# A polynomial-sketch attention with a multiplicative FFN: new float64 conversion, token-major query features and a reordered program

## The chip, the cores and the metric

The kernel runs on one core of one Trainium2 chip. The metric is the device time of one execution in microseconds (us); for a kernel run several times, the median of its runs. Engines: PE is TensorE's matmul, PEld its weight load, DVE is VectorE, ACT is ScalarE, POOL is GpSimd, SP is SyncE, which issues all DMAs here (SPq is its queue).

## The reference

Two parts. The attention maps each query and key x of 32 numbers to 64 features, the outer product of S1 x and S2 x (8 each); with kv = sum of features(k) times v over the tokens and z = sum of features(k), each token and head gets x = (features(q) kv) / (features(q) z + 1e-6). There are 4 batches, 4 heads, 1088 tokens. The four heads of 32 side by side are the 128 numbers of a token for the FFN.

```python
def phi(x):
    a = np.einsum('rd,bhsd->bhsr', S1, x)
    b = np.einsum('rd,bhsd->bhsr', S2, x)
    return np.einsum('bhsi,bhsj->bhsij', a, b).reshape(*x.shape[:-1], r * r)
q_p, k_p = (phi(q), phi(k))
kv = np.einsum('bhsf,bhsd->bhfd', k_p, v)
z = np.sum(k_p, axis=2)
num = np.einsum('bhsf,bhfd->bhsd', q_p, kv)
den = np.einsum('bhsf,bhf->bhs', q_p, z)[..., None] + 1e-06
...
a = x @ w1
b = x @ w2
h = a * b @ w3
return (h @ w_out).astype(np.float32)
```

x is 4352 x 128; w1 and w2 are 128 x 1024, w3 is 1024 x 1024, w_out 1024 x 128. S1, S2 and the four weights arrive as float64; q, k, v are float32. The denominator is a sum with signs that can nearly cancel, so the kernels carry it in pairs of float32 (a leading part on a coarse grid, exact in products and sums, and the rest).

## The kernel before, in words

Tokens are cut into 9 groups: two of 512 for each batch (`q_main`), and one of 256 with the last 64 tokens of each batch (`q_rest`). Since no nonlinearity stands between w3 and w_out, w3o = w3 w_out is computed once (`w3_t` transposes w3 on TensorE, `w3_mm` multiplies by w_out), and a group's FFN is 8 column steps: a product with w1 (`mlp_steps`, L592), ScalarE's copy to SBUF, a product with w2 (L596), VectorE's product of both (ab, L598), and three steps (LAG) later the product with w3o (L605), summed over the 8 steps; then ScalarE copies it (ob), TensorE transposes it (ps_ot), and it is stored.

The weights are loaded as 64-bit words in 22 chunks of 128 x 512 (raw, 4 buffers) in the order w_out, w3, w1, w2. `split_words` (L200 to L220) makes float32 of a chunk: ScalarE scales the low words (L209), VectorE masks, clips, shifts and joins the high words (L211 to L216, six steps), GpSimd multiplies (L217) and `convert` adds the two parts on GpSimd (L306).

Keys, for each batch (`k_steps`): 8 chunks of 128 tokens in two halves of four, and the remaining 64 tokens. For each half TensorE transposes the keys (ps_kt), ScalarE copies (kT), TensorE multiplies by S1 and S2 (ps_ab), VectorE forms the features (kp, L376). `gram` then issues for each chunk two products of kp with v (L412), and three products of the keys' leading part k1 and rest k2 (L416 to L418). `fin1` to `fin3` turn the sums into the matrix M of the denominator, in small VectorE steps between small products (ps_T, ps_M).

Queries, for each group (`q_steps`), with tokens along the free axis: transposes (qT); leading part q1 and rest q2 (GpSimd, L501); two feature products (ps_w, L510) with ScalarE's copy and VectorE's product qp (L523); M q in three products (ps_y, L532 to L534); VectorE's split of it and four GpSimd steps (L540 to L543); numerator and denominator (ps_nd, L552 to L555), the reciprocal between two VectorE transposes, and x (xT).

The program is one list of steps: `merge` interleaves streams by their given costs, and a scheduler then orders each engine's queue. Before the first FFN group stand keys of batches 0 and 1, queries of batch 0 and all of the weights; each batch's two FFN groups are merged with the keys two batches on and the queries one batch on. PSUM: three banks (tag h) for the FFN and the weights, one (t) for transposes, one for the key sums, two (w2) for the queries, one for the FFN's sum.

Of the kernel before, what the change touches and what calls it, by code (L numbers as in the profile page):

```python
# [713 lines left out]
```

## Time and profile before

| what | us |
|---|---|
| median of 3 runs | 427.97 |
| lowest and highest run | 427.85 and 437.18 |
| span of the profiled execution | 425.6 |
| PE busy in it | 356.6 |
| DVE busy | 250.5 |
| POOL busy | 138.3 |
| ACT busy | 98.2 |

The span runs from the first to the last instruction of the profiled execution; the runs' times are those of whole executions and lie 2.4 us above it. Busy times overlap, so they don't add up to the span.

### The profile page before, as it was taken

To read this page: it belongs to the slowest core of one execution; us is meant where nothing else is said; L and a number is where in the kernel's file an instruction comes from. 1 tells how busy PE (TensorE), PEld (TensorE's weight loads), DVE (VectorE), ACT (ScalarE), POOL (GpSimd) and SP (SyncE) were. 2 spreads that over 40 slices of the span, in tenths; PEclk is the share of its full clock that TensorE was granted. 3 is DMA by queue.
4 is the path that set the end of the run, shared out by engine and by line. 5 is a ranking of instruction groups with operands and counts; after the bars stand their busy time and mean duration, and the time that the engine had idled before them with its cause. 6 is when DMAs were issued, how large, how long until landed. Compare 5 with 4: busy or idle time off the path is not lost.

```text
span 425.6 us, 4174 instructions
## 1 busy us (share of the span) xinstructions
PE 356.6 (84%) x1432; PEld 210.7 (50%) x1432; DVE 250.5 (59%) x552; ACT 98.2 (23%) x176; POOL 138.3 (33%) x106
## 2 busy tenths in 40 slices
PE   0665645738788398999999999999999999999994
PEld 0465644626588234364645464464544444445563
DVE  5994499956978997446255643516744554424321
ACT  1212013412032131204211311411221411322231
POOL 0666195394637457051050131104014113002000
PEclk9995658668988689999999999999999999999998
DMA  5986083240227030003000000000000000000001
GB/s 113 259 150 207 12 223 98 65 147 1 69 81 199 1 49 0 2 0 49 26 0 0 2 25 0 0 26 0 0 27 1 0 25 2 0 25 0 26 0 37
DMA packets 44116, 20.71 MB, mean 49 GB/s; under 512 B 37184, under 2 KB 40512, under 8 KB 44096
## 3 DMA queue, kind: packets, MB, share of 16 engines
q1 hardware_dynamic: 44096, 20.46, 18.9%
q8 instruction: 11, 0.18, 0.2%
q14 instruction: 9, 0.07, 0.1%
HBM read 18.22 MB, written 2.23 MB: 48 GB/s over the span
## 4 chain that ended last, share of the span: by engine, by line
PE 70%; DVE 14%; SPq 6%; issue 4%; POOL 4%; ACT 1%; DMA 1%; POOLq 0%; DVEq 0%
PE b_ps L596 14%; PE ps_o L605 14%; PE a_ps L592 14%; PE ps_w L510 4%; SPq L100 4%; PE ps_kvz L412 2%; DVE cv_c L211 2%; PE ps_y L533 2%; DVE cv_a L214 2%; PE ps_w3o L332 2%; DVE cv_a L215 2%; PE ps_y L534 2%; PE ps_nd L554 2%; PE ps_kvz L416 2%; PE ps_ab L368 2%
## 5 line engine op out<-in xcount | busy, mean ns | idle before, releaser
L598 DVE TENSOR_TENSOR ab<-ffa,b_ps 128x512 f32<-128x512 f32 (+1 forms) x72 | 47.2, 656 | 68.5 <-PE b_ps L596 63.5
L592 PE MATMUL a_ps<-xT,w 128*128 128x512 f32 (+1 forms) x144 | 71.8, 580 | 1.2 <-POOL w L306 1.2
L596 PE MATMUL b_ps<-xT,w 128*128 128x512 f32 (+1 forms) x144 | 70.9, 574 | 0.0
L92 ACT COPY ffa<-a_ps 128x512 f32<-128x512 f32 (+1 forms) x72 | 40.5, 563 | 119.5 <-PE a_ps L592 117.5
L605 PE MATMUL ps_o<-ab,w3o 128*128 128x512 f32 (+1 forms) x144 | 67.4, 571 | 0.0
L217 POOL TENSOR_TENSOR cv_m<-cv_m,cv_c 128x512 f32<-128x512 f32 (+1 forms) x23 | 37.2, 1622 | 43.6 <-DVE cv_c L216 26.1
L324 PE MATMUL ps_wt<-ident,w3c 128*128 128x128 f32 x64 | 14.2, 350 | 36.7 <-POOL w3c L306 36.7
L605 PEld LDWEIGHTS ps_o<-ab,w3o 128*128 128x128 f32 x144 | 27.0, 190 | 30.3 <-issue 28.5
L596 PEld LDWEIGHTS b_ps<-xT,w 128*128 128x128 f32 x144 | 27.0, 192 | 28.0 <-issue 27.1
L501 POOL TENSOR_TENSOR q<-qT,q 128x512 f32<-128x512 f32 (+1 forms) x9 | 12.4, 1381 | 84.3 <-DVE q L235 67.4
L540 POOL TENSOR_TENSOR p<-q,yh 128x512 f32<-128x512 bf16 (+1 forms) x9 | 10.0, 1112 | 86.0 <-DVE yh L235 86.0
L592 PEld LDWEIGHTS a_ps<-xT,w 128*128 128x128 f32 x144 | 24.9, 190 | 25.6 <-issue 19.3
L324 PEld LDWEIGHTS ps_wt<-ident,w3c 128*128 128x128 f32 x64 | 9.7, 182 | 39.6 <-POOL w3c L306 39.6
L209 ACT ACTIVATE cv_m<-raw 128x512 f32<-128x512 uint32 x22 | 14.6, 677 | 63.2 <-POOL w3c L306 58.1
L227 DVE TENSOR_REDUCE g_y<-ps_y 128x1 f32<-128x512 f32 (+1 forms) x9 | 5.9, 661 | 31.5 <-PE ps_y L534 31.5
L412 PE MATMUL ps_kvz<-v_sb,kp 128*128 128x64 f32 x128 | 20.3, 287 | 4.5 <-DVE kp L376 4.5
L332 PE MATMUL ps_w3o<-wo,w3T 128*128 128x128 f32 x128 | 23.0, 348 | 0.0
L412 PEld LDWEIGHTS ps_kvz<-v_sb,kp 128*128 128x128 f32 x128 | 19.5, 216 | 6.6 <-DVE kp L376 5.2
L332 PEld LDWEIGHTS ps_w3o<-wo,w3T 128*128 128x128 f32 x128 | 21.9, 260 | 0.5 <-issue 0.5
L306 POOL TENSOR_TENSOR w3c<-cv_a,cv_m 128x512 f32<-128x512 f32 x16 | 21.6, 1353 | 1.0
L392 POOL TENSOR_TENSOR k<-k_sb,k 128x512 f32<-128x512 f32 x8 | 10.3, 1304 | 27.8 <-DVE k L235 27.8
L214 DVE SCALAR_TENSOR_TENSOR cv_a<-cv_c,cv_a 128x512 int32<-128x512 int32 (+1 forms) x23 | 18.6, 818 | 0.0
(167 smaller groups left out, 559.6 us busy)
## 6 DMA issues: line engine op xcount, KB each, us to landing
raw<-in_moe_w_dram SPq DMA_DIRECT2D x20, 512.0 KB, 4.0
k_sb<-in_k_dram SPq DMA_DIRECT2D x16, 128.0 KB, 3.7
v_sb<-in_v_dram SPq DMA_DIRECT2D x4, 512.0 KB, 4.9
q_sb<-in_q_dram SPq DMA_DIRECT2D x16, 128.0 KB, 3.8
out_dram<-oT SPq DMA_DIRECT2D x8, 256.0 KB, 2.0
raw<-in_moe_w_out_dram SPq DMA_DIRECT2D x2, 512.0 KB, 4.8
kr<-in_k_dram SPq DMA_DIRECT2D x4, 32.0 KB, 2.3
vr<-in_v_dram SPq DMA_DIRECT2D x4, 32.0 KB, 2.7
```

The source lines that it names most:

```text
L92: nc.scalar.copy(dst, src)
L100: nc.sync.dma_start(t[:, :, h], bass.AP(tensor=src.tensor, offset=(b * H + h) * S * D, ap=[[NJ * D, 128], [D, NJ], [1, D]]))
L214: nc.vector.scalar_tensor_tensor(a, ci, 0x40000000, a, ALU.bitwise_and, ALU.bitwise_or)
L217: nc.gpsimd.tensor_mul(m, m, c)
L306: nc.gpsimd.tensor_add(dst, hi_f, m)
L324: nc.tensor.transpose(ps[:, c], w3c[:, c * 128:(c + 1) * 128], ident)
L332: nc.tensor.matmul(ps, t[:, c], wo[:, c], start=(c == 0), stop=(c == NC - 1))
L412: nc.tensor.matmul(kv_ps[:, p], kp_chunk[rows, 2 * p:2 * p + 2].rearrange("s h i j -> s (h i j)"), vt[rows, 2 * p:2 * p + 2], start=first ...
L592: nc.tensor.matmul(a_ps[:, :n], w1[:, cols], xT[key], start=True, stop=True)
L596: nc.tensor.matmul(b_ps[:, :n], w2[:, cols], xT[key], start=True, stop=True)
L598: nc.vector.tensor_mul(ab[:, :n], a_sb[:, :n], b_ps[:, :n])
L605: nc.tensor.matmul(s["o"][:, :n], w3o[:, c], s["ab"].pop(c)[:, :n], start=c == 0, stop=c == NC - 1)
```

## The change

`split_words` with its six VectorE steps stays for S1 and S2 alone. The weights get a conversion of their own:

```python
    def convert(n, dst):
        lo, hi = halves(raw.pop(n), CW)
        ...
        nc.scalar.mul(c, hi.bitcast(F32), 2.0 ** -112)
        nc.scalar.mul(m, lo.bitcast(U32), 2.0 ** -29)
        top = HI_TOP * 2.0 ** -112
        nc.vector.tensor_scalar(c, c, top, -top, ALU.min, ALU.max)
        ci = c.bitcast(I32)
        nc.vector.tensor_scalar(t, ci, 3, 0x7FFFFFF8, ALU.logical_shift_left, ALU.bitwise_and)
        nc.vector.scalar_tensor_tensor(t, ci, -(1 << 31), t, ALU.bitwise_and, ALU.bitwise_or)
        nc.vector.tensor_tensor(dst.bitcast(I32), t, m, ALU.add)
        load_raw(n + 1 + NRAW)
```

[...] raw has 6 buffers, and the chunks come in the order w1, w2, w_out, w3.

```diff
-        v_sb[b] = io.tile([128, H, NJ, D], F32, tag="v", name="v_sb")
-        nc.sync.dma_start(v_sb[b].rearrange("p h j d -> p h (j d)"),
-                          bass.AP(tensor=v.tensor, offset=b * H * S * D,
-                                  ap=[[NJ * D, 128], [S * D, H], [1, NJ * D]]))
+        v_sb[b] = io.tile([128, NJ, H, D], F32, tag="v", name="v_sb")
+        load_main(v_sb[b], v, b)
```

So v is loaded as k is, in four DMAs of runs of 32 numbers. Keys: the leading part k1 is bfloat16, GpSimd makes the sum ks = k + k1, and one product of k2 and ks stands for two:

```diff
-                nc.tensor.matmul(kv_ps[:, p],
-                                 kp_chunk[rows, 2 * p:2 * p + 2].rearrange("s h i j -> s (h i j)"),
-                                 vt[rows, 2 * p:2 * p + 2],
+                nc.tensor.matmul(acc["kv"][64 * p:64 * (p + 1)], vt[rows, 2 * p:2 * p + 2].rearrange("p h d -> p (h d)"),
+                                 kp_chunk[rows, 2 * p:2 * p + 2].rearrange("s h i j -> s (h i j)"),
...
-            nc.tensor.matmul(g2_ps, k1[rows], k2[rows], start=False, stop=False, skip_group_check=True)
-            nc.tensor.matmul(g2_ps, k2[rows], kf[rows], start=False, stop=last, skip_group_check=True)
+            nc.tensor.matmul(acc["g2"], k2[rows], ks[rows], start=False, stop=last, skip_group_check=True)
```

Queries: `ay` has the queries as weights (128 tokens at a time, q1 in bfloat16, q2 and qT in float32) and 64 to 96 columns that hold S1, S2 and the key sums of the denominator, so that tokens lie along the partitions. `split` and `dens` form the denominators and 1/den in VectorE steps of 128 to 256 elements per partition, `phi` the features with 1/den in them, `phT` transposes them (8 transposes of 128, ScalarE's copy pT), and `nd` multiplies by kv (ps_x, two products side by side) and ScalarE copies x. The fused FFN functions are as before but for LAG, which is 10 steps counted over all groups, and the order:

```diff
-    run(merge(rest_steps(0, "t") + k_steps(0, "t") + q_main(0, 0, "t") + k_steps(1, "t") + q_main(0, 1, "t"),
-              setup_steps()))
...
+    run(merge(rest_steps(0) + k_steps(0) + q_main(0, 0), weight_steps(("w1", "w2"))))
+    w_st = weight_steps(("wo", "w3"))
+    cut = len(w_st) // 2
+    run(merge(ffn_steps(0), q_main(0, 1), w_st[:cut]))
+    run(merge(ffn_steps(1), k_steps(1) + q_main(1, 0), w_st[cut:]))
+    run(merge(ffn_steps(2), q_main(1, 1), rest_steps(1) + k_steps(2)))
```

SP's queue, from its start: s_raw are the sketches, kr and vr the remaining tokens, raw the words of the weights. Before:

```order
L161 DMA s_raw<-in_S_dram 8x32 x2
L100 DMA k_sb<-in_k_dram 128x8x32 x4
L115 DMA v_sb<-in_v_dram 128x4x256
L105 DMA kr_67<-in_k_dram 64x4x32 x2
L105 DMA vr_71<-in_v_dram 64x4x32 x2
L157 DMA raw<-in_moe_w_out_dram 128x4x128 x2
L100 DMA q_sb<-in_q_dram 128x8x32 x4
L157 DMA raw<-in_moe_w_dram 128x512 x2
```

Now:

```order
L144 DMA s_raw<-in_S_dram 8x32 x2
L85 DMA k_sb<-in_k_dram 128x8x32 x4
L85 DMA v_sb<-in_v_dram 128x8x32 x4
L90 DMA kr_67<-in_k_dram 64x4x32 x2
L90 DMA vr_71<-in_v_dram 64x4x32 x2
L85 DMA q_sb<-in_q_dram 128x8x32 x4
L140 DMA raw<-in_moe_w_dram 128x512 x4
L140 DMA raw<-in_moe_w_out_dram 128x4x128 x2
L85 DMA k_sb<-in_k_dram 128x8x32 x4
```

The words of w1 and w2 come first among the weights, but all raw words now stand behind q, and v is four DMAs instead of one.

TensorE's queue where the FFN starts. Before, with ps_wt and ps_w3o (w3's transposes and products) ahead of the first a_ps, and ps_T and ps_M of key batch 1 around it:

```order
L324 MATMUL ps_wt<-ident,w3c 128x128 x2
L332 MATMUL ps_w3o<-wo,w3T 128x128 x6
L257 MATMUL ps_T<-P1s,gb 128x32
L332 MATMUL ps_w3o<-wo,w3T 128x128 x2
L592 MATMUL a_ps<-xT,w_73 128x512
L255 MATMUL ps_M<-Ta,Pl_blk 128x32
L256 MATMUL ps_M<-Tb,Pl_blk 128x32
L257 MATMUL ps_M<-Ts,Pr_blk 128x32
L496 MATMUL ps_qt<-ident,q_sb 128x128 x4
```

Now, from the first query group's transposed features (ps_ph) and x (ps_x) on:

```order
L584 MATMUL ps_ph<-ident,ph 128x128 x8
L602 MATMUL ps_x<-pT,kz_406 64x512 x2
L498 MATMUL ps_qt<-ident,q_sb 128x128 x4
L646 MATMUL a_ps<-xT,w_73 128x512
L650 MATMUL b_ps<-xT,w_74 128x512
L646 MATMUL a_ps<-xT,w_73 128x512
L650 MATMUL b_ps<-xT,w_74 128x512
L327 MATMUL ps_wt<-ident,w3c 128x128 x4
```

The first FFN products stand ahead of every w3 transpose, behind key batch 0 and one query group alone.

VectorE's queue at a conversion. Before, two chunks at a time, between kp and the next key step:

```order
L376 TENSOR_TENSOR kp<-ps_ab,b_sb 128x1024
L211 TENSOR_SCALAR cv_c<-raw 128x512 x2
L212 TENSOR_SCALAR cv_c<-cv_c 128x512 x2
L213 TENSOR_SCALAR cv_a<-cv_c 128x512 x2
L214 SCALAR_TENSOR_TENSOR cv_a<-cv_c,cv_a 128x512 x2
L215 SCALAR_TENSOR_TENSOR cv_a<-raw,cv_a 128x512 x2
L216 TENSOR_SCALAR cv_c<-cv_a 128x512 x2
L235 TENSOR_SCALAR k_387<-k_sb,g_kb 128x512
```

Now, after the first kp (ISA is the integer add, whose rows count half-words):

```order
L383 TENSOR_TENSOR kp<-ps_ab,b_sb 128x1024
L212 TENSOR_SCALAR cv_c<-cv_c 128x512
L214 TENSOR_SCALAR cv_t<-cv_c 128x512
L215 SCALAR_TENSOR_TENSOR cv_t<-cv_c,cv_t 128x512
L216 ISA w_73<-cv_t,cv_m 128x1024
L212 TENSOR_SCALAR cv_c<-cv_c 128x512
L214 TENSOR_SCALAR cv_t<-cv_c 128x512
L215 SCALAR_TENSOR_TENSOR cv_t<-cv_c,cv_t 128x512
```

Six steps per chunk became four, one of them of a new kind; nine of the 22 adds stand ahead of the FFN's first step on this queue.

## Rows read from the trace of the kernel before

**Rows 1.** Stretches: us, busy us (x instructions) by engine, PEclk, DMA share, GB/s.
```profile
30.00:75.00 45.00, 23.19 (x124) 21.53 (x124) 33.52 (x62) 8.73 (x16) 26.63 (x18) 0.65 0.48 133
75.00:150.00 75.00, 50.36 (x297) 41.51 (x299) 61.95 (x129) 18.63 (x35) 43.69 (x30) 0.80 0.28 78
150.00:419.00 269.00, 267.83 (x938) 134.43 (x934) 130.24 (x269) 64.17 (x112) 54.87 (x47) 1.00 0.05 12
```

**Rows 2.** Waits from 0 to 150 us: who for whom, us in total, times, longest.
```profile
ACT cv_m L209 <- POOL w3c L306: 58.1, 13, 19.0
PE ps_wt L324 <- POOL w3c L306: 36.7, 11, 10.1
```

**Rows 3.** Time line of PE, first FFN product: start, us, what (x instructions).
```profile
151.64 1.06 PE L596 MATMUL b_ps<-xT,w 128*128 128x512 f32 x1
```

**Rows 4.** Time line of PE at the full clock, 238 to 262 us.
```profile
238.59 0.60 PE L496 MATMUL ps_qt<-ident,q_sb 128*128 128x128 f32 x4
239.02 1.02 PE L592 MATMUL a_ps<-xT,w 128*128 128x512 f32 x2
...
240.50 1.13 PE L510 MATMUL ps_w<-qT,Sa 64*128 64x512 f32 x4
241.56 1.10 PE L368 MATMUL ps_ab<-S12blk,kT 128*128 128x64 f32 x8
242.50 1.08 PE L596 MATMUL b_ps<-xT,w 128*128 128x512 f32 x2
...
250.48 0.55 PE L412 MATMUL ps_kvz<-v_sb,kp 128*128 128x64 f32 x4
250.87 0.44 PE L416 MATMUL ps_kvz<-k 128*128 128x128 f32 x2
251.15 0.39 PE L417 MATMUL ps_kvz<-k,k 128*128 128x128 f32 x2
251.37 0.39 PE L418 MATMUL ps_kvz<-k_sb,k 128*128 128x128 f32 x2
251.59 0.56 PE L412 MATMUL ps_kvz<-v_sb,kp 128*128 128x64 f32 x4
...
258.38 1.02 PE L596 MATMUL b_ps<-xT,w 128*128 128x512 f32 x2
259.24 1.02 PE L605 MATMUL ps_o<-ab,w3o 128*128 128x512 f32 x2
260.19 1.08 PE L552 MATMUL ps_nd<-qp,kz 128*64 128x512 f32 x4
261.20 1.13 PE L554 MATMUL ps_nd<-p,ones_blk 128*128 128x512 f32 x2
```

**Rows 5.** Time line of DVE from 20 to 126 us, with and without GpSimd beside.
```profile
20.66 1.22 DVE L376 TENSOR_TENSOR kp<-ps_ab,b_sb 128x1024 f32<-128x1024 f32 x1
...
108.69 1.48 DVE L216 TENSOR_SCALAR cv_c<-cv_a 128x512 int32<-128x512 int32 x1
...
124.20 0.42 DVE L211 TENSOR_SCALAR cv_c<-raw 128x512 int32<-128x512 int32 x1
124.54 0.42 DVE L213 TENSOR_SCALAR cv_a<-cv_c 128x512 int32<-128x512 int32 x1
...
125.21 0.68 DVE L214 SCALAR_TENSOR_TENSOR cv_a<-cv_c,cv_a 128x512 int32<-128x512 int32 x1
125.81 0.42 DVE L213 TENSOR_SCALAR cv_a<-cv_c 128x512 int32<-128x512 int32 x1
```

**Rows 6.** Group of instructions by line: busy us, mean ns of one, idle before.
```profile
L458 DVE TENSOR_TENSOR gb<-gb,g 128x128 f32<-128x128 f32 x4 | 1.1, 284 | 0.1
```

**Rows 7.** Time line of SPq, the first issues: start, us, what.
```profile
1.53 3.45 SPq L100 DMA_DIRECT2D k_sb<-in_k_dram  x4
5.02 0.67 SPq L115 DMA_DIRECT2D v_sb<-in_v_dram  x1
```

**Rows 8.** Time line of PE, the last FFN products.
```profile
417.49 1.89 PE L605 MATMUL ps_o<-ab,w3o 128*128 128x256 f32 x8
```

More of the change, by code (lines that the diff above doesn't have):

```diff
@@ L20 @@
 EPS = 1e-6
-GRP = 512
 CW = 512
-LAG = 3
-NRAW = 4
+LAG = 10
+NRAW = 6
 def f32_of_bits(bits):
@@ L332, in w3_mm @@
                 nc.tensor.matmul(ps, t[:, c], wo[:, c], start=(c == 0), stop=(c == NC - 1))
-            copy(w3o[:, ko], ps, DM, "act")
+            nc.scalar.copy(w3o[:, ko], ps)
         for n, (name, i) in enumerate(chunks):
+            if name not in which:
+                continue
             if name == "wo":
@@ L497, in tr, with lead_q @@
             s["qT"] = wtile("qT", bufs=2)
-            copy(s["qT"], ps[:, :n], n)
+            nc.scalar.copy(s["qT"], ps[:, :n])
+            if after:
+                after()
+        st.append((0.5, tr))
+        def lead_q():
             s["q1"], s["q2"] = wtile("q1", BF16), wtile("q2")
@@ new lines, in q_steps @@
+        st.append((0.9, phT))
+        def nd():
+            ps = psum.tile([128, 512], F32, tag="t", name="ps_x")
+            merged = []
+            for j, part in enumerate(parts):
+                for (b, c0, nn) in part:
+                    c0 += j * 128
+                    if merged and merged[-1][0] == b and merged[-1][1] + merged[-1][2] == c0:
+                        merged[-1][2] += nn
+                    else:
+                        merged.append([b, c0, nn])
+            for (b, c0, nn) in merged:
+                for p in range(2):
+                    nc.tensor.matmul(ps[64 * p:64 * (p + 1), c0:c0 + nn], kz_done[b][:, 64 * p:64 * (p + 1)],
+                                     s["pT"][:, p, c0:c0 + nn], start=True, stop=True)
+            xT[key] = wtile("xT", bufs=3)
+            nc.scalar.copy(xT[key], ps[:, :n])
@@ L629, in mlp_main, with main_dst @@
-    def mlp_main(b, half):
+        return q_steps(lambda: srcs, "rest", [[(2 * m + i, i * SR, SR) for i in range(2)] for m in range(2)])
+    def main_dst(b, half):
         def dst(oT):
@@ new lines, with ffn_ab @@
+    groups = [((b, half), 512, main_dst(b, half)) for b in range(B) for half in range(2)]
+    groups.append(("rest", 2 * 128, rest_dst))
+    NG = len(groups)
+    ab_sb, o_ps = {}, {}
+    def ffn_ab(g, c):
+        key, n, _ = groups[g]
+        cols = slice(c * 128, (c + 1) * 128)
+        a_ps = psum.tile([128, 512], F32, tag="h", bufs=3, name="a_ps")
+        nc.tensor.matmul(a_ps[:, :n], w1[:, cols], xT[key], start=True, stop=True)
+        a_sb = work.tile([128, 512], F32, tag="ffa", name="ffa")
+        nc.scalar.copy(a_sb[:, :n], a_ps[:, :n])
+        b_ps = psum.tile([128, 512], F32, tag="h", bufs=3, name="b_ps")
+        nc.tensor.matmul(b_ps[:, :n], w2[:, cols], xT[key], start=True, stop=True)
+        ab = work.tile([128, 512], F32, tag="ab", bufs=LAG + 2, name="ab")
+        nc.vector.tensor_mul(ab[:, :n], a_sb[:, :n], b_ps[:, :n])
+        ab_sb[g, c] = ab
@@ new lines, in ffn_o, with ffn_out @@
+    def ffn_o(g, c):
+        _, n, _ = groups[g]
+        if c == 0:
+            o_ps[g] = psum.tile([DM, 512], F32, tag="out", name="ps_o")
+        nc.tensor.matmul(o_ps[g][:, :n], w3o[:, c], ab_sb.pop((g, c))[:, :n], start=c == 0, stop=c == NC - 1)
+        if c == NC - 1:
+            o_ps[g, "sb"] = work.tile([DM, 512], F32, tag="ob", bufs=1, name="ob")
+            nc.scalar.copy(o_ps[g, "sb"][:, :n], o_ps[g][:, :n])
+    def ffn_out(g):
+        _, n, dst = groups[g]
+        ps = psum.tile([128, 4, DM], F32, tag="h", bufs=3, name="ps_ot")
+        nj = n // 128
+        for j in range(nj):
+            nc.tensor.transpose(ps[:, j], o_ps[g, "sb"][:, j * 128:(j + 1) * 128], ident)
+        oT = work.tile([128, 4, DM], F32, tag="oT", name="oT")
+        nc.scalar.copy(oT[:, :nj], ps[:, :nj])
+        dst(oT)
@@ L646, in merge, with ffn_steps, o_step @@
+    def ffn_steps(g):
+        st = []
+        for c in range(NC):
+            w = groups[g][1] / 512
+            st.append((1.7 * w, lambda c=c: ffn_ab(g, c)))
+            i = g * NC + c - LAG
+            if i >= 0:
+                st += o_step(i)
+        return st
+    def o_step(i):
+        g, c = divmod(i, NC)
+        st = [(0.85, lambda: ffn_o(g, c))]
+        if c == 1 and g:
+            st.append((0.5, lambda: ffn_out(g - 1)))
+        return st
     def merge(*streams):
```

500 lines of the change are left out of this document (226 added, 274 removed).

## The prediction

> **What bounds the kernel now.** I read the table by stretches first. It splits the run in two [rows 1]. From 150 to 419 us TensorE is busy for 267.8 of 269 us at the full clock (1.00, which is 2.4 GHz): nothing but TensorE's own work counts there. From 30 to 150 us it is busy for 23.2 of 45 and 50.4 of 75 us, at a mean clock of 0.65 and 0.80, so it waits and part of the time runs at 1.2 GHz. Then I looked up who is waited for in the first 150 us [rows 2]: the weight transposes wait 36.7 us for GpSimd's last step of a conversion, and ScalarE's first step of the next one waits 58.1 us for the same. The chain of float64 conversions (ScalarE, six VectorE steps, two GpSimd steps, 22 chunks) paces this part, and the FFN stands behind it: its first product with w2 starts at 151.6 us [rows 3]. So 150 us are half used, then 269 us are full, then 6 us of tail (425.6 less 419.4, the end of the last FFN products [rows 8]).
>
> **Prices.** I take the distance from one start to the next in the time line at full clock, since matmuls overlap [rows 4]. A float32 product of 512 columns: 259.24 less 258.38 = 0.86 us. Four 128-column transposes: 0.43, so 0.11 each. Four 64-column products (ps_ab): 0.94, so 0.235 each. One pair of half-height feature products (ps_w): 1.06. Two column halves side by side (ps_nd from qp and kz): 1.01. One key chunk: 0.39 (kp with v) + 0.28 + 0.22 + 0.22 = 1.11. On VectorE [rows 5] a one-source step on 512 float32 takes 0.33 and a two-source step 0.60 when starts are compared (124.20 to 124.54, 125.21 to 125.81); 1024 elements take 1.13 of such distance (1.22 as duration, kp). The same one-source step takes 1.48 (108.69) while GpSimd converts.
>
> **The change, part by part.**
> (1) Conversion. Old: six VectorE steps, 4 x 0.33 + 2 x 0.60 = 2.5 us undisturbed, but the row with 1.48 shows steps held more than threefold beside GpSimd. New: two one-source steps, one two-source step and an integer add that writes 1024 half-words; GpSimd does none. The add has no row. Below, it costs a 512-element two-source step, 0.60; above, I take twice the 1024-element one, 2.3. It writes 1024 elements, so I take 1.13: 2 x 0.33 + 0.60 + 1.13 = 2.4 us per chunk. ScalarE does two steps instead of one; it was busy for 18.6 of 75 us [rows 1], so I cost that at nothing while it runs ahead.
> (2) Keys. Per chunk the two products of kp and v now have the 64 columns of v as weights, stand in different column halves and run side by side: 0.22 x 1.01 / 0.86 = 0.26 (0.44 if they don't overlap). The bfloat16 square is between a quarter of 0.22 and all of it, and I take half, 0.11, and one product with the sum of parts replaces two: 0.22. That is 0.59 against 1.11 (bounds 0.54 and 0.88). A batch of 9 chunks: 5.3, plus 8 transposes 0.9, 8 ps_ab 1.9, small products 1.3 = 9.4 us.
> (3) Queries. Old per group: 0.43 + 2 x 1.06 + 2 x 0.86 + 0.2 (bfloat16, no row; a quarter of 0.86 as an estimate) + 1.01 + 2 x 0.95 = 7.4 us. New: transposes 0.43, four times (bfloat16 0.11 + two float32 products with 64 and 96 columns, both priced as ps_ab, 0.235) = 2.3 (1.9 to 2.8), eight transposes 0.9, the side-by-side pair 1.0: 4.6 us. VectorE per group: about 30 steps, from 0.2 (128 elements, 0.284 as duration [rows 6]) to 0.60, together 6.5 us. GpSimd keeps one subtraction of its five steps. New waits stand in TensorE's queue: the products ay wait for that subtraction, the transposes of the features for VectorE's last step, the product x for ScalarE's copy; behind each stand FFN products, which then wait too. In the new order 1.7 to 8 us of FFN products lie between each such pair, so I charge nothing in steady state; without that cover it is up to 7 us per group.
> (4) Loads. v comes in four DMAs of 128-byte runs. As k it then costs 3.45 us of issue for 512 KB against 0.67 [rows 7], so kr, q and the weight words come 2.8 us later in the first stretch; kr was not waited for before, and I charge nothing, 3 us as upper bound. The Trainium skill (DMA: Bandwidth & Descriptors, Specifications) asks for runs of at least 512 bytes for line rate, and this speaks against the change: by the rule v costs as much as k, by bytes alone nothing. The issue rows agree with the rule; by it the sum would be 2.8 us longer.
> (5) Order. w1 and w2 are converted first and the FFN starts as soon as the first x is there; w3's transposes and products go below groups 0 and 1; the products with w3o lag ten steps behind, so that they need not wait.
>
> **The sum.** Stretch P, to the first x. Up to the first kp all is as before: it ends at 20.66 + 1.22 = 21.9 [rows 5]. From there VectorE does, in its new order, 9 conversions 21.6, one kp 1.1, the lead parts of key batch 1 and a maximum of batch 2 4.5, some 35 small steps of 0.2 7, the query steps 6.5: 41 us. It waits about 9 us for others (products of the second half at the low clock, 4 x 1.2; ps_ay 3; GpSimd's subtraction 1). After the last step of it: transposes, two ScalarE copies and a product, 3.5 us. 21.9 + 41 + 9 + 3.5 = 75 us, where it was 150.
> Stretch W, groups 0 and 1 with w3. TensorE: 16 x 2 x 0.86 = 27.5, six products with w3o 5.2, 64 transposes 7.0, 64 products of w3 14.1, two query groups 8.8, key batch 1 9.4 = 72 us. VectorE: 13 conversions 31, 16 products ab 9.6, two query groups 13, keys 8, lead of batch 2 2.3 = 64 us. Two engines that are both nearly full and wait for each other through three PSUM buffers lose some 10%: 80 us.
> Stretch R, the rest. The FFN is 24 x (8 x 0.86 + 0.43) = 175.4 in all, 142.7 of it left; 5 query groups and the half one 25.4; batches 2 and 3 with the remainder 19.2; outputs 34 x 0.11 = 3.7: 191 us. VectorE has about 90 us of work here (52 products ab 31, five and a half query groups 36, two key batches some 20), so TensorE is the bound as it was from 150 to 419 us, and I add 4 us for waits at the seams of the groups.
> 75 + 80 + 191 + 4 + 6 (tail) = 356 us of span. The profiled run's span was 425.6 and the median of the runs 427.97, so 2.4 lie around it: 359 us.
> The same prices on the old kernel from 150 us (175 + 3.7 + 7.5 x 7.4 + two batches of 14 = 262) give 98% of the 267.8 that the row shows.
>
> **Rivals.**
> TensorE at 1.2 GHz in W. For it: at 52% busy the mean clock was 0.65, at 67% 0.80 [rows 1], and W has TensorE waiting for VectorE. Against: in W TensorE has 72 of 80 us to do, more than in either row, and half clock fills its own gaps. If half of W's products run at half clock: 36 us more, 395 us. The Trainium skill (TensorE: Matmul & The Clock Gate, Why this matters for your kernels) warns that an idle gap between bursts takes the clock back to 1.2 GHz; the rows at 0.65 and 0.80 agree with that.
> The FFN doesn't start early. ScalarE runs its queue in order, and the new conversions put two steps on words that are now loaded behind v and q; kT, b_sb, pT and xT stand between them. If raw words or the three buffers of cv_c hold ScalarE, P grows by what [rows 2] shows for one such chain, about 30 us: 389 us.
> Slower: the integer add. Each us that it costs above 1.13 adds 9 us to P and, once W's spare 15 us are used, 13 us to W. At 3.8 us extra (5 us per add) the gain is gone, at 4.5 the time is 359 + 9 x 4.5 + 13 x 4.5 - 15 = 443 us. For it: it is the one step without any row. Against: no VectorE step of the trace with 1024 elements needs over 1.3 us.
>
> **How the numbers follow.** The forecast 0.82, the clock 0.07, the late start 0.08, the slow add 0.03. Lower end: add at 0.60 (5 us off P) and W bound by TensorE alone (72) with a start some 5 us sooner: 343. Upper end: add at 2.3 (11 on P, a few on W) and chunks at 0.88 (8 us), up to just short of the late start: 388. That leaves out about 2 in 10. A change under 2% (419 to 436 us) can't be told from none here. Faster 0.95, within 2% 0.02, slower 0.03.
>
> **What would show it.** In the profile after: first FFN product at about 75 us (65 to 85 is right, over 100 is the second rival); the last w3 product at about 155; L216 near 1.1 us; VectorE's one-source steps near 0.42 all through; a stretch with TensorE at 1.00 clock and no gaps from 155 us to the end; key chunks near 0.6 and query groups near 4.6 us of TensorE. I am wrong if TensorE has gaps of over 10% after 160 us, or if the mean clock of W is under 0.8.

## The result and the profile after

The changed kernel takes 361.26 us (median of 4 runs, 360.90 to 361.73), the kernel before 428.33 in the same comparison: a ratio of 0.8436, with a 95% interval of 0.8423 to 0.8449. One of the four runs before, at 437.18 us, is left out of the ratio. The forecast was 359.0. The profiled execution has a span of 359.1 us. All times of experiments below are medians, and the ratios behind them are to the kernel before on the same chip (427.7 to 428.0 us).

First the stretches of the kernel after, with the columns of [rows 1] (us; busy of PE, PEld, DVE, ACT, POOL; granted clock, DMA share, GB/s):

```profile
30.00:75.00 45.00, 19.77 (x83) 13.86 (x83) 34.15 (x98) 12.20 (x20) 3.85 (x3) 0.50 0.74 166
75.00:150.00 75.00, 73.90 (x416) 49.05 (x415) 54.42 (x130) 34.95 (x66) 4.44 (x3) 0.97 0.27 64
150.00:353.00 203.00, 200.27 (x837) 108.19 (x835) 99.16 (x272) 57.94 (x105) 9.65 (x7) 1.00 0.05 14
```

Before, TensorE was half used until 150 us; now it is half used until 75 us and full from there. GpSimd, busy for 43.7 us of the second stretch before, has 4.4 left. The head of the FFN in TensorE's time line (start, us, what; answers to [rows 3]):

```profile
68.42 1.94 PE L584 MATMUL ps_ph<-ident,ph 128*128 128x128 f32 x8 [8.67 <-DVE ph L577]
71.46 1.98 PE L602 MATMUL ps_x<-pT,kz 128*64 128x512 f32 x4 [1.10 <-ACT pT L587]
74.12 1.11 PE L498 MATMUL ps_qt<-ident,q_sb 128*128 128x128 f32 x4 [0.69 <-ACT xT L605]
75.03 1.92 PE L646 MATMUL a_ps<-xT,w 128*128 128x512 f32 x2
```

The first FFN product starts at 75.0 us, but it takes twice what the same products take later: the granted clock from 30 to 80 us is 0.50, which is 1.2 GHz, after a stretch in which TensorE waited most of the time. The waits of the first 150 us (answer to [rows 2]):

```profile
PE ps_ph L584 <- DVE ph L577: 8.7, 1, 8.7
...
PE ps_kt L366 <- DMA kr<-in_k_dram: 3.4, 1, 3.4
```

The two waits for GpSimd's last conversion step (58.1 and 36.7 us) are gone. What is left is short and spread: TensorE waits 8.7 us once for VectorE's features, 6.1 us at the start for the sketches, 4.2 and 3.9 us within the small products of key batch 0, and 3.4 us for the keys of the remainder, which SP's queue loads behind v (answer to [rows 7]):

```profile
1.54 3.05 SPq L85 DMA_DIRECT2D k_sb<-in_k_dram  x4
4.63 3.21 SPq L85 DMA_DIRECT2D v_sb<-in_v_dram  x4
7.89 1.61 SPq L90 DMA_DIRECT2D kr<-in_k_dram  x2
```

The conversion's steps by line (count | busy us, mean ns; answer to [rows 5]; CUSTOM_DVE_ANT_0 is the integer add):

```profile
L215 DVE SCALAR_TENSOR_TENSOR cv_t<-cv_c,cv_t 128x512 int32<-128x512 int32 x22 | 15.8, 723 | 0.3
L216 DVE CUSTOM_DVE_ANT_0 w3c<-cv_t,cv_m 128x1024 uint16<-128x1024 uint16 x16 | 12.1, 757 | 0.4 <-PE ps_wt L327 0.2
L214 DVE TENSOR_SCALAR cv_t<-cv_c 128x512 int32<-128x512 int32 x22 | 9.1, 419 | 0.2
L212 DVE TENSOR_SCALAR cv_c<-cv_c 128x512 f32<-128x512 f32 x22 | 9.0, 421 | 5.8 <-ACT cv_c L209 5.8
```

The one-source steps (L212, L214) take 0.42 us as mean over all 22 chunks, where the same kind took 0.42 undisturbed and up to 1.48 before. At full clock, the first product of a query group's ay and the first work behind them, an FFN product, and a key chunk with the start of the next, in TensorE's time line (answer to [rows 4]):

```profile
162.42 0.19 PE L518 MATMUL ps_ay<-Rh,q 128*128 128x64 bf16 x1
...
164.71 0.60 PE L366 MATMUL ps_kt<-ident,k_sb 128*128 128x128 f32 x4
...
168.62 1.02 PE L650 MATMUL b_ps<-xT,w 128*128 128x512 f32 x2
169.57 0.44 PE L415 MATMUL ps_kvz<-kp,v_sb 128*64 128x128 f32 x4
169.94 0.23 PE L418 MATMUL ps_kvz<-k 128*128 128x128 bf16 x1
170.01 0.44 PE L419 MATMUL ps_kvz<-ks,k 128*128 128x128 f32 x2
170.38 0.44 PE L415 MATMUL ps_kvz<-kp,v_sb 128*64 128x128 f32 x4
```

The last products of w3, the transposes of a query group's features behind them and, at the end, the last FFN products in the same view (answers to [rows 8]), and the add in VectorE's:

```profile
149.12 1.95 PE L335 MATMUL ps_w3o<-wo,w3T 128*128 128x128 f32 x16
...
153.48 1.04 PE L584 MATMUL ps_ph<-ident,ph 128*128 128x128 f32 x8
...
350.36 2.75 PE L659 MATMUL ps_o<-ab,w3o 128*128 128x256 f32 x12
```

```profile
62.02 0.68 DVE L216 CUSTOM_DVE_ANT_0 w3c<-cv_t,cv_m 128x1024 uint16<-128x1024 uint16 x1
62.63 0.42 DVE L543 TENSOR_TENSOR ay_h<-ps_ay,g_ay 128x256 f32<-128x256 f32 x1
```

From start to start, the add takes 0.61 us, a key chunk takes 170.38 less 169.57 = 0.81 us, against 1.11 before, and the four parts of ay 164.71 less 162.42 = 2.29.

### The profile page after: what moved, and what is told of

Its sections match the earlier page's. It is cut to its first block, busy times and chain, and to the rows that moved or that the text cites. A ratio compares the mean times of both kernels' runs of the same rounds, so it can differ in the third digit from the quotient of the medians.

```text
span 359.1 us, 4019 instructions
## 1 busy us (share of the span) xinstructions
PE 309.2 (86%) x1404; PEld 182.1 (51%) x1404; DVE 207.1 (58%) x575; ACT 115.4 (32%) x211; POOL 22.3 (6%) x21
## 3 DMA queue, kind: packets, MB, share of 16 engines
q1 hardware_dynamic: 58624, 20.46, 25.4%
## 4 chain that ended last, share of the span: by engine, by line
PE 80%; DVE 9%; SPq 3%; ACT 2%; DMA 2%; POOL 1%; issue 1%; DVEq 0%; POOLq 0%; ACTq 0%
PE ps_o L659 16%; PE a_ps L646 16%; PE b_ps L650 15%; PE ps_kvz L415 4%; PE ps_w3o L335 4%; PE ps_kvz L419 3%; PE ps_ay L523 3%; PE ps_x L602 3%; PE ps_ay L525 3%; PE ps_ph L584 2%; PE ps_ab L375 2%; SPq L85 2%; PE ps_wt L327 2%; PE ps_kvz L418 2%; DMA k_sb<-in_k_dram 2%; POOL q L508 1%
## 5 line engine op out<-in xcount | busy, mean ns | idle before, releaser
L646 PE MATMUL a_ps<-xT,w 128*128 128x512 f32 (+1 forms) x144 | 72.6, 587 | 0.0
L648 ACT COPY ffa<-a_ps 128x512 f32<-128x512 f32 (+1 forms) x72 | 40.5, 562 | 82.9 <-PE a_ps L646 82.9
L659 PEld LDWEIGHTS ps_o<-ab,w3o 128*128 128x128 f32 x144 | 25.5, 190 | 24.7 <-issue 20.5
L415 PE MATMUL ps_kvz<-kp,v_sb 128*64 128x128 f32 x128 | 16.2, 335 | 3.3 <-DVE kp L383 3.3
L419 PE MATMUL ps_kvz<-ks,k 128*128 128x128 f32 (+1 forms) x72 | 18.5, 344 | 0.0
L209 ACT ACTIVATE cv_c<-raw 128x512 f32<-128x512 f32 x22 | 14.7, 674 | 11.3 <-DVE cv_t L215 8.0
L523 PE MATMUL ps_ay<-Rf,q 128*128 128x64 f32 (+1 forms) x72 | 15.0, 301 | 3.4 <-POOL q L508 3.4
L584 PE MATMUL ps_ph<-ident,ph 128*128 128x128 f32 x68 | 10.0, 290 | 8.7 <-DVE ph L577 8.7
L396 POOL TENSOR_TENSOR ks<-k_sb,k 128x1024 f32<-128x1024 f32 x4 | 10.6, 2651 | 95.2 <-DVE k L232 95.2
L215 DVE SCALAR_TENSOR_TENSOR cv_t<-cv_c,cv_t 128x512 int32<-128x512 int32 x22 | 15.8, 723 | 0.3
L210 ACT ACTIVATE cv_m<-raw 128x512 int32<-128x512 uint32 x22 | 14.7, 675 | 3.0 <-DVE w3c L216 2.6
L525 PE MATMUL ps_ay<-Rl,qT 128*128 128x96 f32 (+1 forms) x72 | 15.0, 302 | 0.0
L584 PEld LDWEIGHTS ps_ph<-ident,ph 128*128 128x128 f32 x68 | 8.6, 150 | 12.6 <-issue 12.3
```

Of the source, the lines that this page charges most:

```text
L215: nc.vector.scalar_tensor_tensor(t, ci, -(1 << 31), t, ALU.bitwise_and, ALU.bitwise_or)
L415: nc.tensor.matmul(acc["kv"][64 * p:64 * (p + 1)], vt[rows, 2 * p:2 * p + 2].rearrange("p h d -> p (h d)"), kp_chunk[rows, 2 * p:2 * p + 2 ...
L419: nc.tensor.matmul(acc["g2"], k2[rows], ks[rows], start=False, stop=last, skip_group_check=True)
L523: nc.tensor.matmul(C[rows, j, :64], s["q2"][:, cols], Rf[:, b].rearrange("p x h i -> p (x h i)"), start=True, stop=False, skip_group_check ...
L525: nc.tensor.matmul(C[rows, j], s["qT"][:, cols], Rl[:, b].rearrange("p x h i -> p (x h i)"), start=False, stop=True, skip_group_check=True)
L584: nc.tensor.transpose(ps[:, p, j * 128:(j + 1) * 128], s["ph"][:, j, 2 * p:2 * p + 2].rearrange("p h i j -> p (h i j)"), ident)
```

## The experiments

A kernel's span is TensorE's busy time plus its idle time, so the first line of each page (busy us of PE) against the span tells which of the two an edit moved. Spans are those of the profiled executions; for all new parts, weights first, that one was the slowest of four (357.0 us), so its span is some 1 us above what the median suggests.

| kernel | time, us | span | PE busy | PE idle |
|---|---|---|---|---|
| before | 428 | 425.6 | 356.6 | 69.0 |
| new conversion alone | 378.2 | 375.9 | 343.3 | 32.6 |
| all new parts, weights first | 355.9 | 355.3 | 309.6 | 45.7 |
| after (all new parts, early FFN) | 361.3 | 359.1 | 309.2 | 49.9 |
| after with the old conversion | 386.0 | 383.6 | 313.7 | 69.9 |
| the same, weights first | 398.2 | 395.8 | 319.8 | 76.0 |

(A chunk count of 26 stands in some expectations; the kernel has 22, as the rows above show.)

**Conversion alone, on the kernel before.**

```diff
-            hi_f, m = split_words(*halves(raw.pop(n), CW), 128, CW)
-            nc.gpsimd.tensor_add(dst, hi_f, m)
...
+            nc.scalar.mul(c, hi.bitcast(F32), 2.0 ** -112)
+            nc.scalar.mul(m, lo.bitcast(U32), 2.0 ** -29)
...
+            nc.vector.tensor_tensor(dst.bitcast(I32), t, m, ALU.add)
```

> The kernel before with only the new conversion: two ScalarE and four VectorE steps per chunk of weights, no GpSimd step; keys, queries, loads and order as in the kernel before. Output as before. The front of the kernel before ends at 151.6 us with its first w2 product, and its weight transposes wait 36.7 us for GpSimd's last conversion step. My theory: the conversion paces that front, and with 22 chunks at some 1.5 us less each it gets 30 to 40 us shorter: 388 to 398 us. Rival, keys and queries hold the front just as much (GpSimd's query steps, VectorE's key steps), so the conversion alone gives under 15 us: over 413 us.

Measured 378.23 us (0.8846, 0.8823 to 0.8869): 49.6 us less, beyond what I expected, and three quarters of the whole gain, with the order, the keys, the queries and the loads of the kernel before. From its page:

```profile
PE 343.3 (91%) x1432; PEld 199.7 (53%) x1432; DVE 210.7 (56%) x508; ACT 109.7 (29%) x198; POOL 65.3 (17%) x62
```

TensorE's idle time fell from 69.0 to 32.6 us, and its busy time by 13.3 with the same 1432 instructions; a stretch of its front, to be read beside [rows 1]:

```profile
30.00:75.00 45.00, 36.04 (x236) 31.09 (x235) 34.71 (x87) 23.72 (x46) 8.13 (x7) 0.85 0.71 215
```

TensorE is busy for 36.0 us of it instead of 23.2, and the granted clock is 0.85 instead of 0.65, so the same products also take less. The first product of the FFN with w1 moved from 139.7 us (the row in [rows 3] is the first with w2, 12 us later) to 96.7, 43.0 of the 49.6 us:

```profile
139.74 1.12 PE L592 MATMUL a_ps<-xT,w 128*128 128x512 f32 x2 [1.21 <-POOL w L306]
...
96.69 1.02 PE L604 MATMUL a_ps<-xT,w 128*128 128x512 f32 x2
```

The rival is out. The edit both drops steps and takes GpSimd out of the chain; what each is worth is estimated with the next run.

**Old conversion in the changed kernel.**

```diff
-        nc.scalar.mul(c, hi.bitcast(F32), 2.0 ** -112)
...
-        nc.vector.tensor_tensor(dst.bitcast(I32), t, m, ALU.add)
...
+        nc.vector.tensor_scalar(ci, a, -(1 << 23), None, ALU.bitwise_and)
+        nc.gpsimd.tensor_mul(m, m, c)
+        nc.gpsimd.tensor_add(dst, a.bitcast(F32), m)
```

> The changed kernel, with the 26 weight chunks converted by the old steps (one ScalarE, six VectorE, two GpSimd steps) in the new order. Output as before. My theory: the conversion paces the first 75 us and is a price of its own, since VectorE's steps are stretched beside GpSimd's (changed kernel 0.42 us for a one-source step, kernel before 0.52 to 0.8 on average). Nine chunks of the first part then cost some 2 us more each (18 us) and the 17 of the next part some 1.5 us more, half of it hidden: 380 to 396 us, first FFN product at 90 us or later. Rival, the order alone brought the gain and the steps stand beside other work: within 5 us of 361.

Measured 385.98 us (0.9023, 0.9007 to 0.9038): 24.7 more than the changed kernel, as expected; the first FFN product came at 83.8 us, sooner than the 90 I expected. Three of its groups:

```profile
L214 DVE SCALAR_TENSOR_TENSOR cv_a<-cv_c,cv_a 128x512 int32<-128x512 int32 x22 | 22.1, 1003 | 0.0
L211 DVE TENSOR_SCALAR cv_c<-raw 128x512 int32<-128x512 int32 x22 | 21.7, 986 | 0.9 <-DMA raw<-in_moe_w_dram 0.9
L213 DVE TENSOR_SCALAR cv_a<-cv_c 128x512 int32<-128x512 int32 x22 | 11.1, 505 | 0.0
```

With GpSimd back in each chunk, the first one-source step of VectorE (L211) takes 0.99 us as mean, against 0.42 undisturbed in [rows 5]; the three others take 0.44 to 0.51. The two-source steps take 1.00 and 0.84, against 0.68 there. VectorE's six steps come to 94.2 us in the whole kernel, where the four new ones take 50.1. Undisturbed, by [rows 5], the six would take 22 x (4 x 0.42 + 2 x 0.68) = 67 us, so by this estimate some 17 us of the difference are the fewer steps and 27 the stretching. How the 24.7 us divide between the two isn't shown.

**The add on GpSimd.**

```diff
-        nc.vector.tensor_tensor(dst.bitcast(I32), t, m, ALU.add)
+        nc.gpsimd.tensor_tensor(dst.bitcast(I32), t, m, ALU.add)
```

> The changed kernel with the last step of each conversion, the integer add, on GpSimd instead of VectorE. Output as before. It takes 26 x 0.6 us off VectorE. My theory: what made the old conversion slow is GpSimd beside VectorE, so the one-source steps go from 0.42 to 0.6 us or more, each chunk ends only after a GpSimd step of 1 to 3 us, and the first FFN product comes at 80 to 90 us: 366 to 380 us. Rival, VectorE's own work is what paces, and relief helps: 352 to 359 us, with the first FFN product at 70 us or sooner.

Measured 365.28 us (0.8526, 0.8497 to 0.8554): 4.0 more, so taking the add off VectorE is a loss. Groups:

```profile
L216 POOL TENSOR_TENSOR w3c<-cv_t,cv_m 128x512 int32<-128x512 int32 x16 | 22.0, 1379 | 49.6 <-PE ps_wt L327 29.3 <-DVE cv_t L215 8.6 <-DVE g_ay L539 5.5
...
L214 DVE TENSOR_SCALAR cv_t<-cv_c 128x512 int32<-128x512 int32 x22 | 14.6, 666 | 6.9 <-POOL w3c L216 6.2
```

VectorE's busy time fell by 1.1 us only, from 207.1 to 206.0, though the adds had taken 16.2 of it: L214 alone went from 0.42 to 0.67 us, which gives back 5.4, and each chunk now ends after a GpSimd step of 1.4. The total is just under the range I gave. The first FFN product came at 74.1 us, sooner than I expected, so the loss falls behind it:

```profile
75.00:150.00 75.00, 70.37 (x393) 46.36 (x392) 50.41 (x109) 34.24 (x64) 22.29 (x16) 0.98 0.31 78
```

TensorE is busy for 70.4 us of the second stretch, 3.5 less than in the changed kernel, which is most of the 4.0.

**Weights first.**

```diff
-    run(merge(rest_steps(0) + k_steps(0) + q_main(0, 0), weight_steps(("w1", "w2"))))
-    w_st = weight_steps(("wo", "w3"))
-    cut = len(w_st) // 2
-    run(merge(ffn_steps(0), q_main(0, 1), w_st[:cut]))
-    run(merge(ffn_steps(1), k_steps(1) + q_main(1, 0), w_st[cut:]))
+    run(merge(rest_steps(0) + k_steps(0) + q_main(0, 0) + k_steps(1) + q_main(0, 1), weight_steps(("w1", "w2", "wo", "w3"))))
+    run(merge(ffn_steps(0)))
+    run(merge(ffn_steps(1), q_main(1, 0)))
```

> The changed kernel with all new parts, but in the old order: all 26 conversions, both key batches 0 and 1 and three query groups are laid before the first FFN product. Output as before. My theory: the same work is done, and only what stood beside the FFN products moves in front of them: first FFN product at 110 to 125 us, then a stretch that TensorE fills; the total rises only by the extra time in which TensorE idles in front, some 30 us of 115 less what the W part lost to waits: 375 to 390 us. Rival A, the cheaper steps are the gain and the order does nothing: within 5 us of 361. Rival B, the early start is nearly all of the gain: over 400 us.

Measured 355.90 us (0.8315, 0.8299 to 0.8330): 5.4 us faster than the changed kernel. Both my theory and its rival B fall, and rival A has the place almost right, though the order does do something: in this kernel the early FFN costs. TensorE here, up to its first FFN product at 105.6 us:

```profile
30.00:105.60 75.60, 54.49 (x367) 44.57 (x367) 62.13 (x156) 34.87 (x68) 7.75 (x4) 0.98 0.67 155
```

The FFN starts 30.6 us later, yet TensorE idles less ahead of it: 15.4 us up to 30 and 21.1 behind, 36.5, against 15.3 + 25.2 = 40.5 in the changed kernel. The products of w3 and of key batch 1 fill gaps in the front; in the changed kernel they are done later, by a TensorE that has no gaps to give. The second query group, which the edit lists ahead too, was scheduled behind the first FFN product: 20 of the two groups' 40 rows of ay stand ahead of 105.6 us. The clock's 0.98 in this row doesn't hold for the whole front, as 16 rows of w3's products show:

```profile
57.19 3.62 PE L335 MATMUL ps_w3o<-wo,w3T 128*128 128x128 f32 x16
...
69.44 2.00 PE L335 MATMUL ps_w3o<-wo,w3T 128*128 128x128 f32 x16
```

So TensorE ran at half rate here too, but early, and was back at full rate well ahead of the FFN.

**Old conversion, weights first** (the two edits above together).

> The changed kernel with the old conversion and, besides, all weights, both first key batches and three query groups laid before the FFN, as in the kernel before. Output as before. With the cheap conversion the old order was 5 us faster (355.9 against 361.3); with the old conversion in the new order 386.0 was measured. My theory: the early FFN start hides a slow conversion under FFN products and is worth something only then, so that this kernel needs 15 to 30 us more than 386: 400 to 416 us. Rival, the order is worth the same with either conversion: 379 to 384 us.

Measured 398.18 us (0.9307, 0.9289 to 0.9326): 12.2 more than with the early FFN. So the order's worth depends on the conversion: an early FFN gives 12 us while conversions are slow and takes 5 once they are quick. By the table, the 12 us are half idle time (69.9 instead of 76.0: the conversions' waits stand beside FFN products) and half busy time for the same products (313.7 instead of 319.8). The size is under what I expected, the sign is mine and against the rival.

**Old key products.**

```diff
-                nc.tensor.matmul(acc["kv"][64 * p:64 * (p + 1)], vt[rows, 2 * p:2 * p + 2].rearrange("p h d -> p (h d)"),
-                                 kp_chunk[rows, 2 * p:2 * p + 2].rearrange("s h i j -> s (h i j)"),
+                nc.tensor.matmul(acc["kv"][:, 64 * p:64 * (p + 1)], kp_chunk[rows, 2 * p:2 * p + 2].rearrange("s h i j -> s (h i j)"),
+                                 vt[rows, 2 * p:2 * p + 2].rearrange("p h d -> p (h d)"),
...
-        nc.vector.tensor_sub(k2, kf, k1)
-        nc.gpsimd.tensor_add(ks, kf, k1)
+        nc.gpsimd.tensor_sub(k2, kf, k1)
...
+            nc.tensor.matmul(acc["g2"], k1[rows], k2[rows], start=False, stop=False, skip_group_check=True)
```

k1 is float32 again, and the sum ks falls away.

> The changed kernel with the old key products: feature products with v in one group of 128 rows by columns of the accumulator, a float32 leading part, and two products for the cross term instead of one with the sum of parts. The numerator sums then lie transposed for what reads them, so the numerators are not the reference's. The trace of the changed kernel has a key chunk at full clock at 0.81 us from one start to the next, against 1.11 in the kernel before. My theory: TensorE is full from 75 us on, so 27 chunks at 0.30 bring 8 us there, and nine more at half clock in the first part up to 5: 369 to 374 us. Rival, key chunks stand in gaps of TensorE: under 2 us.

Measured 368.05 us (0.8595, 0.8575 to 0.8614): 6.8 more, 1 us under the range I gave. One of its chunks, with the start of the next:

```profile
171.79 0.56 PE L414 MATMUL ps_kvz<-v_sb,kp 128*128 128x64 f32 x4
...
172.69 0.39 PE L419 MATMUL ps_kvz<-k_sb,k 128*128 128x128 f32 x2
172.91 0.56 PE L414 MATMUL ps_kvz<-v_sb,kp 128*128 128x64 f32 x4
```

1.12 us per chunk against 0.81: 27 chunks behind the FFN's start make 8.4 us, of which 6.8 are seen, so the rival (gaps) is out.

**v in one DMA**, on the kernel with the old key products, which read v in either layout.

```diff
-        v_sb[b] = io.tile([128, NJ, H, D], F32, tag="v", name="v_sb")
-        load_main(v_sb[b], v, b)
+        v_sb[b] = io.tile([128, H, NJ, D], F32, tag="v", name="v_sb")
+        nc.sync.dma_start(v_sb[b].rearrange("p h j d -> p h (j d)"),
+                          bass.AP(tensor=v.tensor, offset=b * H * S * D, ap=[[NJ * D, 128], [S * D, H], [1, NJ * D]]))
```

> The changed kernel with the old key products (as in the run with those alone, 368.1 us) and, besides, v loaded per batch in one DMA with runs of 1 KB, as in the kernel before; v is the moving operand there, so that its layout may be strided. The numerators again lie transposed for what reads them. To be set against the run with old key products. My theory: v's four DMAs with 128-byte runs put the rows of the remainder, q and the weight words 2.5 us later, and the first stretch begins with these rows, so one DMA gives 2 to 4 us: 364 to 366 us. Rival, the transfers stand beside other work: 367 to 369 us.

Measured 369.50 us (0.8626, 0.8607 to 0.8646) against 368.05: no gain; the intervals overlap. My theory falls. The head does start sooner, the transposes of the first 512 keys at 11.6 us instead of 13.6, but the first FFN product comes at 72.6 instead of 73.1. What is not shown is whether this would hold with the new key products, which were run with v in four DMAs alone.

**Remainder ahead of v.**

```diff
-    load_k(0)
+    k_sb[0] = io.tile([128, NJ, H, D], F32, tag="k", name="k_sb")
+    load_main(k_sb[0], k, 0)
     load_rest(k_rs[0], k, 0)
     load_rest(v_rs[0], v, 0)
+    v_sb[0] = io.tile([128, NJ, H, D], F32, tag="v", name="v_sb")
+    load_main(v_sb[0], v, 0)
```

> The changed kernel with the loads of the remainder's keys and values issued ahead of the four DMAs of v. Output as before. In the changed kernel TensorE waits 3.4 us and VectorE 1.9 us for the remainder's keys in the first 15 us. My theory: these waits are the head of the first stretch, and it starts 2 to 3 us sooner: 358 to 359.5 us. Rival, what follows waits for v, q or the weight words instead: 361 us, no difference.

Measured 356.30 us (352.44 to 357.32; 0.8314, 0.8282 to 0.8346): 5.0 us faster, more than the 2 to 3 us that I expected. The first FFN product comes earlier by as much:

```profile
70.12 1.91 PE L649 MATMUL a_ps<-xT,w 128*128 128x512 f32 x2
```

70.1 against 75.0 us. The waits for the remainder explain a part: the transposes of the first 512 keys start 2.3 us sooner (11.36 against 13.63). At VectorE's second kp it is 4.0 us, in the changed kernel and here:

```profile
27.66 1.22 DVE L383 TENSOR_TENSOR kp<-ps_ab,b_sb 128x1024 f32<-128x1024 f32 x1
...
23.69 1.23 DVE L386 TENSOR_TENSOR kp<-ps_ab,b_sb 128x1024 f32<-128x1024 f32 x1 [1.46 <-ACT b_sb L382]
```

Between the first kp and this one VectorE did nine conversion steps in the changed kernel and does three here. So the edit also moved the program's order on VectorE, and which of the two gives the 5 us isn't separated; with v in one DMA the same head start of 2 us left 0.5.

**Added products, early and late.** First seven products of 512 columns, which nothing ties to a place in the queue:

```diff
+        for i in range(7):
+            nc.tensor.matmul(ps, ident, w1[:, :512], start=True, stop=True)
...
+    q0.insert(3, (0.0, warm))
```

> The changed kernel with seven more products of 512 columns in TensorE's queue, behind the first query group's products ay and ahead of its feature transposes, where TensorE waits 8.7 us for VectorE. They write a PSUM bank that nobody reads before the FFN overwrites it; the output is as before. In the changed kernel the granted clock is 0.50 from 30 to 80 us, and the transposes, the product x and the first FFN products run at half rate (first FFN product 1.06 us where later ones take 0.59). My theory: weights first is 5 us faster because its TensorE is at full rate when the FFN starts. Then the seven products lift the clock before the transposes, these take 0.9 instead of 1.9 us, the x pair 1.0 instead of 2.0, and 5 us of FFN products at half rate are saved by half: 355 to 358 us. Rival, the 5 us come from more overlap of VectorE's work and the clock costs nothing: 360 to 362 us; if the added products end after VectorE's last step they delay the transposes: 362 to 366 us.

Measured 357.93 us (0.8363, 0.8350 to 0.8377), 3.3 less. The number fits my theory, the place does not: the program's scheduler laid the seven products between 25 and 38 us.

```profile
28.12 2.79 PE L717 MATMUL ps_warm<-w,ident 128*128 128x512 f32 x6
```

There they lifted the rate of the second half of key batch 0, whose chunks take 0.81 us from start to start instead of 1.38. The 8.7 us gap and the transposes at half rate were still there, 1.7 us earlier (66.74 us). The first four FFN products then took 4.4 us instead of 5.8, which makes 3.1 of the 3.3 us.

So a second kernel ties the first product to a value of the query group:

```diff
+                nc.tensor.matmul(ps[:, :32], ident, g, start=True, stop=True)
+                for _ in range(5):
+                    nc.tensor.matmul(ps, ident, w1[:, :512], start=True, stop=True)
```

> The changed kernel with one product of 32 columns that reads the first query group's grid, and behind it five of 512 columns into the same unread bank. In the run with seven added products the program's scheduler had laid them at 25 to 38 us, where they gave 3.3 us; here the first one needs a value that VectorE writes at 62 us, so they stand in the 8.7 us gap ahead of the feature transposes. Output as before. My theory: TensorE is back at full rate at 66 us; transposes 0.9 instead of 1.9 us, the x pair 1.0 instead of 2.0, and the FFN products of 75 to 80 us take half: 4 to 5 us less than 361.3, so 356 to 357.5 us. Rival, the rate has no part in it: 361 us.

Measured 358.49 us (0.8381, 0.8366 to 0.8395), 2.8 less, not 4 to 5:

```profile
62.33 6.20 PE L550 MATMUL ps_warm<-w,ident 128*128 128x512 f32 x10
68.36 1.11 PE L589 MATMUL ps_ph<-ident,ph 128*128 128x128 f32 x8
70.58 1.08 PE L607 MATMUL ps_x<-pT,kz 128*64 128x512 f32 x4 [1.10 <-ACT pT L592]
72.34 0.99 PE L498 MATMUL ps_qt<-ident,q_sb 128*128 128x128 f32 x4 [0.69 <-ACT xT L610]
73.13 1.92 PE L651 MATMUL a_ps<-xT,w 128*128 128x512 f32 x2
```

The transposes and the x pair now run at full rate, 1.9 us sooner in all, but after two short gaps for ScalarE's copies (1.10 and 0.69 us) the first FFN product is at half rate again; the first four take 4.8 us instead of 5.8. With the 1.9 that makes 2.9, where 2.8 were measured. The low rate is thus a part of what the early FFN loses; that it is all of the 5.4 us isn't shown.

**Two attempts at a best version.**

> The kernel with all weights first (355.9 us), with two changes of the loads: the remainder's keys and values ahead of v (which gave 5 us in the new order), and the loads of batch 1 and of the other remainders behind four more chunks of weight words, for which ScalarE waits up to 13.3 us there. Output as before. My theory: the gains add where both stand in the first stretch: 346 to 351 us. Rival, what the loads give is hidden behind VectorE's conversions, which then end last: 353 to 356 us.

Measured 356.70 us (0.8337, 0.8319 to 0.8354): nothing gained over 355.9; VectorE is busy for all of 30 to 40 us there, as the rival had it. Set beside the early FFN with the remainder ahead of v (356.30), it also shows that the order's 5.4 us are gone once the remainder comes first: the two are the same within their intervals. (This kernel moves batch 1's loads as well; weights first with the remainder alone moved was not run.)

> The changed kernel (early FFN) with the remainder's keys and values ahead of v and the late added products of the run before. Output as before. If the two gains are separate (5 us and 4 to 5 us): 351 to 353 us. If the earlier start already takes the stretch at low rate away: 355 to 357 us.

Measured 353.17 us (349.16 to 353.95; 0.8227, 0.8194 to 0.8261): 8.1 us, 2.2%, under the changed kernel and the fastest of all. It is the changed kernel with two small edits: the remainder loaded ahead of v, and six products that nobody reads. The gains (5.0 and 2.8) add; the runs of this kernel and of the one with the remainder ahead of v spread by some 5 us each, those of the others by under 3. Its head of the FFN:

```profile
67.25 1.08 PE L610 MATMUL ps_x<-pT,kz 128*64 128x512 f32 x4 [1.10 <-ACT pT L595]
69.01 0.66 PE L501 MATMUL ps_qt<-ident,q_sb 128*128 128x128 f32 x4 [0.69 <-ACT xT L613]
69.50 1.02 PE L654 MATMUL a_ps<-xT,w 128*128 128x512 f32 x2
```

Here the same two gaps are followed by a product at full rate, so the gaps alone don't decide it.

## Why the prediction came out

The total was right within 2.3 us, in part by luck: the profiled span of 359.1 us is 75.0 + 76 + 202 with 6 behind it, where the sum has 75 + 80 + 195 + 6, and errors inside each stretch cancel too.

- **Stretch P, 75 us: measured 75.0.** The mechanism held: with GpSimd out of the chain, VectorE's steps keep their undisturbed length, but for single ones beside GpSimd's remaining work. Four terms were off, and they cancel. The first kp ended at 19.0 us and not at 21.9 as before. VectorE was then busy for 36.9 of the 50.2 us up to its last feature at 69.2, where I wrote 41: the integer add costs 0.61 us from start to start, my lower bound and not the 1.13 I took, 4.7 us less over nine chunks. The waits were 13.3 us where I wrote 9; two of them (1.3 and 2.5 us) are for ScalarE's first conversion step, which I had put at nothing. And the last transposes and the x pair ran at half rate, 5.8 us from VectorE's last feature to the FFN, where I wrote 3.5. 19.0 + 36.9 + 13.3 + 5.8 = 75.0.
- **W, 80 us: measured 76** (75.0 to the end of the last w3 product, 151.1). TensorE was busy for 73.9 of the 75 us to 150, so the 10% that I charged for two engines waiting for each other didn't occur. Its work was longer than the 72 us I added up: 75.2 from start to start, with 35.0 for the FFN instead of 32.7 (2.4 of it because the first four products ran at half rate) and 11.0 for the keys instead of 9.4. W held both groups' ay, but the transposes and the x pair of one group only.
- **R, 191 + 4: measured 202** (to 353.1). The other group's transposes and x pair, 0.88 + 1.01 = 1.9 us, fell here. The FFN took 147.2 us instead of 142.7: a product that stands alone among other work takes some 0.95 (168.62 to 169.57 above), not 0.86. The keys took 22.0 instead of 19.2, since a chunk takes 0.81 and not 0.59: the two halves of kp with v take 0.37 together (forecast 0.26), and the product with the sum of parts 0.37 (forecast 0.22), though a product of the same shape takes 0.22 in the old chunk. The queries took 26.8 instead of 25.4 with the 1.9, so a group's 4.6 holds: 0.43 + 2.29 + 0.88 + 1.01. With 3.5 for the outputs and 2.7 of idle time that makes 202.2.
- **The rival of TensorE at 1.2 GHz** did not come in W, where the granted clock was 0.97, but in its first 5 us and in P from 30 us on (0.50). There the sum had priced the key products alone at the low clock.
- **The rival of a late FFN start, 389 us, was wrongly built.** It counted each us of delay in full. With the start 30.6 us later the time was 355.9, since the work laid in front is missing behind. The sum came out as P + W + R, but it let the reader believe that the move from 150 to 75 us is the gain. It is not: conversion alone brings 49.6 us in the old order, the other new parts 22.3 on top, and the early FFN takes 5.4 back in the kernel as built.
- **Loads.** That v's four DMAs cost nothing by themselves held, as far as the run with one DMA tells (368.05 against 369.50 us). SP's issue rows for v do differ, 3.12 us in four DMAs against 0.67 in one. The Trainium skill's rule on runs of 512 bytes (DMA: Bandwidth & Descriptors, Specifications), by which, as an estimate, the four would have cost the 2.8 us, goes the way of these rows but is not borne out by the total; no run measures the transfer's rate itself. That the remainder's keys are not waited for did not hold. TensorE waits 3.4 us for them, and loading them first gives 5.0.

The sum also has slips that change little: two query groups are 9.2 us and not 8.8, 356 + 2.4 is 358.4, and the lower end of the range adds up to 341 and not 343.

The other new parts (keys, queries, v's loads, w1 and w2 first among the chunks) took 33.7 us off TensorE's busy time (343.3 to 309.6), and 13.1 of it came back as idle time (32.6 to 45.7). By the profiled spans 20.6 us are left, by the medians 22.3: TensorE has less to do in the front, but the front is not that much shorter. But for the key products and v's loads, these parts were not undone one by one.

## What to carry to other kernels

Split a time into the bound engine's busy and idle parts before pricing a change of order: work moved ahead of a start is not lost if that engine was idle there. In these runs an early start was worth 12.2 us while it put a slow chain under the bound engine's products, and nothing or less once the chain was quick. Take the second engine out of a chain of elementwise steps if its steps stretch the first one's, and look at the few small loads at the head of the queue once the big chain is gone. An estimate that comes out right should still be undone part by part: here the order, which looked like the centre of the change, cost 5.4 us as built, and nothing once the remainder's keys came first (356.3 against 356.7).
